# Side B of a decode-attention kernel: tiles of eight heads in 64 KB rows, one transfer a tile

## The chip, the cores and the metric

The kernel runs on one core of a Trainium2 chip. The metric is the device time of one execution, in microseconds. Before the change the median of three runs is 824.88 us (824.64 to 827.48).

## The reference

Two independent attention layers, A and B, each decode one token for 32 heads of 128 values. The two results of 512 values stand side by side in the output. For each side:

```python
q = (x @ wq) split into 32 heads                 # x: 1 x 512, wq: 512 x 4096
scores = einsum("bhqd,bhkd->bhqk", q, k) * 128 ** -0.5
p = softmax(scores)
o = einsum("bhqk,bhkd->bhqd", p, v)
return o reshaped to 1 x 4096 @ wo               # wo: 4096 x 512
```

Everything is bfloat16. Both caches hold 16384 positions a head. A attends to all of them, B to the last W = 4096 only. So A reads 2 x 134 MB of K and V, B 2 x 33.5 MB, and the four weights add 4.2 MB each.

## The kernel before

**Units.** The work is 20 units in the order B0, A0 to A15, B1 to B3; this text numbers them 0 to 19 by place. A unit has an 8.4 MB tile of K and one of V: 128 partitions, each with 256 positions of 128 values, taken as two halves (u = 0, 1) of CH = 128 positions. There are two K buffers (`KS`, alternating) and one V buffer (`VS`).

On side A a unit is two heads; partitions 0 to 63 hold the first, each 256 positions in a row of 64 KB, and one transfer loads the whole tile (`a_pair`, L292). On side B a unit is eight heads, but as two parts of four (`parts` = 2): half u holds heads 4(2g + u) to 4(2g + u) + 3, with partition p = 4i + h holding 128 positions (block i of 32) of head h in a row of 32 KB (`b_window`, L289). Each half is a transfer of its own. Heads lie 4 MiB apart in memory.

**The steps of a unit.** VectorE multiplies each half of K by the head's query (`scores_prod`, L413), adds the 128 values up in a tree of four halvings (`scores_tree`, L425) and a reduction (`scores_sum`, L432), and takes each partition's maximum (`unit_max`, L441). TensorE turns the maxima into a row; VectorE reduces that to one maximum a head (L464) and spreads it again (L465), and TensorE turns it back to a column (`max_all`, L469). ScalarE takes the exponentials (L492) and spreads p over the heads of the tile, one masked copy for each (`spread_p`, L478). TensorE sums the exponentials (`soft_sum`, L520) and multiplies p by V in 64 matmuls (`pv`, L540); ScalarE normalizes them (`evict`, L552); TensorE and ScalarE bring the result into columns (`columns`, L562 and L571). With two parts, side B does the maxima, turns, exponentials and sums for two columns.

**Order.** It is written out by hand in the loop of L687. Unit T's first product stands ahead of the softmax and P·V of unit T - 1, which are put between the steps of unit T. All big loads are issued by SP, in program order: in unit T first V of T - 1 and then K of T + 1, each when its buffer is free. K's buffer is freed by VectorE (`free_k`, L437), V's by ScalarE's copy at L571. Program order and keys decide the semaphores: `_Stream.op` (L71) adds a wait where an operation reads or writes what another wrote or still reads, and the emission is at L120.

**Start.** ScalarE issues six small loads of x (L658). SP loads B's query weights, the first half of unit 0's K, A's query weights and the other half of K (L661 to L664). `spread_x` (L360) copies x, for each of the `nh` heads of a tile, into its share of a zeroed 128-column weight; `project_q` (L386) multiplies with it in groups of 4 x `nh` matmuls and four slots of the query tile, so that each partition gets the query of its own head. B has two such groups, and the copy of each to `q` (L402) has a key of its own, which `scores_prod` names. TensorE takes A's x (`spread_x(A)`) ahead of B's projection.

**End.** The last unit's V is loaded in halves into a free K buffer and into V's (L698, L729), behind A's output weights; B's output weights come last, in five pieces. A's output is projected while VectorE is still at the last unit (L738). The last unit's P·V goes by columns: `pv_columns` (L575) takes V as the weight and 4 columns of p, 128 matmuls for each part, into two PSUM banks, with a normalization after each. The masks for its second half are VectorE's (L483), those for the first ScalarE's. Then `permute_o` (L592) and `project_out_columns` (L624) give B's output.

Of the kernel before, what the change touches and what calls it, by code (L numbers as in the profile page):

```python
# [9 lines left out]
F32 = mybir.dt.float32  # L10
# [193 lines left out]
def kernel(  # L204
# [19 lines left out]
    DN = A_wo.shape[1]  # L224
    KC = D // P
    inv = 1.0 / math.sqrt(DH)
    assert SkA == P // 2 * 2 * CH and WB == P // 4 * CH

    pool = ctx.enter_context(tc.tile_pool(name="pool", bufs=1))
    psum = ctx.enter_context(tc.tile_pool(name="psum", bufs=1, space=bass.MemoryType.PSUM))  # L230
# [1 line left out]
    def sb(name, shape, dtype):  # L232
        return pool.tile(shape, dtype, tag=name, name=name)
# [4 lines left out]
    def flat(t):  # L238
        return t.rearrange("p l d -> p (l d)")
# [2 lines left out]
    VS = sb("v", [P, 2 * CH, DH], BF16)  # L242
    identf = sb("identf", [P, P], F32)
    ident = sb("ident", [P, P], BF16)
    one_f = sb("one_f", [1, 1], F32)
    one_b = sb("one_b", [1, 1], BF16)
    ones_col = sb("ones_col", [P, 1], F32)
    pick = sb("pick", [HQ, P + 4], BF16)
    sc = sb("sc", [P, 2 * CH], F32)
    m_t = sb("m", [P, 2], F32)  # L250
    M_t = sb("M", [1, 8], F32)
    Mr = sb("Mr", [1, 2 * P], F32)
    bias = sb("bias", [P, 2], F32)
    p_t = sb("p", [P, 2 * CH], BF16)
    cs = sb("cs", [P, 2], F32)
    csm = sb("csm", [P, 8], F32)
    pm_t = sb("pm", [P, 2 * CH * 4], BF16)
    r_t = sb("r", [P, 8], F32)
    osb = sb("osb", [P, 512], F32)
    cols = sb("cols", [P, 4], F32)  # L260
# [3 lines left out]
    OC2 = pst("oc2")  # L264

    A, B = _Side(), _Side()
    for s, n, x, wq, wo, nh in ((A, "A", A_x, A_wq, A_wo, 2), (B, "B", B_x, B_wq, B_wo, 4)):
        s.n, s.x, s.wq, s.wo, s.nh, s.parts = n, x, wq, wo, nh, nh // 2
        s.xT = sb(f"xT{n}", [P, KC], BF16)
        s.q = sb(f"q{n}", [P, HQ // nh, DH], BF16)  # L270
        s.O = sb(f"O{n}", [P, HQ], BF16)
        s.Op = sb(f"Op{n}", [P, HQ], BF16)
        s.mask = sb(f"mask{n}", [P, nh], F32)
        s.groups = 4 // s.parts
        s.rows = sb(f"rows{n}", [P, 8 * s.groups // nh, nh, 4], F32)
        s.sel = sb(f"sel{n}", [P, s.parts, nh * 4], F32)
        s.o = pst(f"o{n}")
# [8 lines left out]
            return ap.rearrange("p (h i) -> p h i", h=s.nh)  # L286
        return ap.rearrange("p (i h) -> p h i", h=s.nh)

    def b_window(cache, g):  # L289
        return cache[0, 4 * g : 4 * g + 4, SkB - WB : SkB, :].rearrange("h (i l) d -> i h (l d)", l=CH)  # L290

    def a_pair(cache, g):  # L292
        return cache[0, 2 * g : 2 * g + 2, :, :].rearrange("h (i l) d -> (h i) (l d)", l=2 * CH)
# [16 lines left out]
    def load(dst, src, w, dma, tok=None):  # L310
        st.op("SP", lambda: L.dma_start(out=dst, in_=src), w=w, dma=dma, tok=tok)  # L311

    def load_k_half(un, u):
        load(flat(un.K[:, u * CH : (u + 1) * CH, :]), b_window(B_k_cache, 2 * un.g + u),
             [f"k{un.k}{u}"], f"K{un.k}{u}")

    def load_k(un):
        if un.s is A:
            load(flat(un.K[:, :, :]), a_pair(A_k_cache, un.g), [f"k{un.k}0", f"k{un.k}1"], f"K{un.k}0")
        else:  # L320
            for u in (0, 1):
                load_k_half(un, u)

    def load_v(un):
        if un.s is A:
            load(flat(VS[:, :, :]), a_pair(A_v_cache, un.g), ["v0", "v1"], "V0", "V0")
        else:
            for u in (0, 1):
                load(flat(VS[:, u * CH : (u + 1) * CH, :]), b_window(B_v_cache, 2 * un.g + u),
                     [f"v{u}"], f"V{u}", f"V{u}")  # L330

    def load_wq(s, W, key):
        s.wq_t, s.wq_key = W, key
# [70 lines left out]
    def scores_prod(un, u):  # L404
        s = un.s
        k = un.K[:, u * CH : (u + 1) * CH, :]
        j = un.g if s is A else 2 * un.g + u
        kk = f"k{un.k}{u}"
        ahead = un.g - st.loop["DVE"][1] if st.loop.get("DVE") else None

        def mul(it=None):
            i = j if it is None else it + ahead
            return V.tensor_tensor(  # L413
                out=k, in0=k, in1=s.q[:, bass.ds(i, 1), :].broadcast_to([P, CH, DH]), op=ALU.mult
            )

        st.op("DVE", mul, r=[kk, f"q{s.n}{j // 4}"], w=[kk],
              takes=[f"K{un.k}{u}"] if s is B or u == 0 else [])

    def scores_tree(un, u):  # L420
        k = un.K[:, u * CH : (u + 1) * CH, :]
# [30 lines left out]
    def max_all(un):  # L452
        s, n = un.s, un.s.parts
        w = n * s.nh
        if s is A:
            rows, wide = by_head(s, sm[0:1, 0:P]), by_head(s, Mr[:, 0:P])
            Mv = M_t[:, 0:w]
            spread = Mv.unsqueeze(2).broadcast_to([1, s.nh, P // s.nh])
        else:
            rows = sm[0:1, 0 : n * P].rearrange("p (v i h) -> p v h i", v=n, h=s.nh)  # L460
            wide = Mr[:, 0 : n * P].rearrange("p (v i h) -> p v h i", v=n, h=s.nh)
            Mv = M_t[:, 0:w].rearrange("p (v h) -> p v h", v=n)
            spread = Mv.unsqueeze(3).broadcast_to([1, n, s.nh, P // s.nh])
        st.op("DVE", lambda it=None: V.tensor_reduce(out=Mv, in_=rows, axis=AX.X, op=ALU.max), r=["sm_r"], w=["M"], takes=["smr"])  # L464
        st.op("DVE", lambda it=None: V.tensor_copy(wide, spread), r=["M"], w=["Mr"], tok="Mr")  # L465

        def turn():
            for v in range(n):
                i = T_.matmul(  # L469
                    sm[:, 256 + v : 257 + v], lhsT=Mr[:, v * P : (v + 1) * P], rhs=one_f[:, :],  # L470
                    start=True, stop=True,
                )
            return i

        st.op("PE", turn, r=["Mr", "one_f"], w=["sm_c"], takes=["Mr"], tok="smc")

    def on_scalar(out, in_, mask):
        return S.activation(out=out, in_=in_, func=ACT.Copy, scale=mask)  # L478
# [53 lines left out]
    def pv(un):  # L532
        s, n, g = un.s, un.n // 4, un.s.groups

        def mms():
            for i in range(n):
                for v in range(s.parts):
                    r0 = 32 * (v * g + i % g)
                    l = v * n + i
                    x = T_.matmul(  # L540
                        s.o[r0 : r0 + un.rows, :],
                        lhsT=un.pm[:, l, :, :].rearrange("p a b -> p (a b)"),
                        rhs=VS[:, 4 * l : 4 * l + 4, :],
                        start=(i < g), stop=(i >= n - g),
                    )
            return x

        st.op("PE", mms, r=["v0", "v1"] + [f"pm0.{j}" for j in range(4)], w=["o" + s.n], takes=["V0"] if s is A else ["V0", "V1"], tok="pv")

    def evict(un):  # L550
        s = un.s
# [20 lines left out]

        st.op("ACT", keep, r=["oc", "v0", "v1"], w=[f"O{s.n}.{un.col(0)}"], takes=["oc"], tok="of")

    def pv_columns(un, v, V_t, vk, ps, pk, pmk, takes):  # L575
        s = un.s

        def mms():
            for l in range(un.n):
                x = T_.matmul(  # L580
                    ps[:, 0 : s.nh], lhsT=V_t[:, l, :], rhs=un.pm[:, (v * un.n + l) // 4, :, l % 4],
                    start=(l == 0), stop=(l == un.n - 1),
                )
            return x

        st.op("PE", mms, r=[vk] + [f"{pmk}.{j}" for j in range(4)], w=[pk], takes=takes)
        st.op("DVE", lambda: V.tensor_tensor(  # L587
            out=s.O[:, un.col(v) : un.col(v) + s.nh], in0=ps[:, 0 : s.nh],
            in1=r_t[:, v * s.nh : (v + 1) * s.nh], op=ALU.mult,
        ), r=[pk, "r"], w=[f"O{s.n}.{un.col(v)}"])  # L590

    def permute_o(s):  # L592
        oT = TP[0][0:HQ, 0 : P // 2].bitcast(BF16)
# [57 lines left out]

    wo_pieces = (16, 8, 4, 3, 1)

    x0 = 4 * KC * P
    for s in (B, A):
        s.x_row = flat(KS[1][0:1, :, :])[:, x0 : x0 + D]
        for a, b in ((0, D // 4), (D // 4, D // 2), (D // 2, D)):
# [9 lines left out]
        out=identf[:, :], in_=identf[:, :], compare_op=ALU.not_equal, fill=1.0, base=0,  # L667
        pattern=[[-1, P]], channel_multiplier=1,
    ), r=["identf0"], w=["identf"])
    for t, key, val in ((one_f, "one_f", 1.0), (one_b, "one_b", 1.0), (ones_col, "ones_col", 1.0),  # L670
                        (A.o, "oA", 0.0), (B.o, "oB", 0.0)):
        st.op("DVE", lambda t=t, val=val: V.memset(t[:, :], val), w=[key])
    st.op("DVE", lambda: V.tensor_copy(ident[:, :], identf[:, :]), r=["identf"], w=["ident"])
    spread_x(B, flat(KS[1][:, :, :]), "k10")
    for s in (B, A):
# [6 lines left out]
    project_q(B)  # L682
    project_q(A)
    st.op("SP", lambda: L.dma_start(out=flat(KS[1][:, :, :]), in_=a_pair(A_k_cache, 0)),
          w=["k10", "k11", "xA", "xB"] + [f"k10.{j}" for j in range(4)], dma="K10")

    for T, un in enumerate(units):  # L687
        prev = units[T - 1] if T >= 1 else None
# [4 lines left out]
        if un.last:  # L693
            W, wk = KS[NT % 2], f"k{NT % 2}"
            s = A
            A.wo_t = flat(W[:, 0:CH, :]).rearrange("p (r f) -> p r f", r=HQ)
            load(A.wo_t[:, :, :], A.wo.rearrange("(p r) f -> p r f", r=HQ), [wk + "0"], "woA0")
            load(flat(W[:, CH : 2 * CH, :]), b_window(B_v_cache, 2 * un.g), [wk + "1"], "VL0")  # L698
        both = prev is not None and prev.s is A and un.s is A and prev.g >= 1
        st.loop["DVE"] = ("A", un.g - un.g % 2) if both else None  # L700
        pe = lambda u: {e: ("A", u.g) if u.s is A else None for e in ("PE", "ACT")}
# [24 lines left out]
            st.end_iteration("DVE")  # L726
        st.loop = {}
    un = units[-1]
    load(flat(VS[:, 0:CH, :]), b_window(B_v_cache, 2 * un.g + 1), ["v0"], "VL1")  # L729
    B.wo_t = flat(VS[:, CH : 2 * CH, :]).rearrange("p (r f) -> p r f", r=HQ)  # L730
    src = B.wo.rearrange("(p r) f -> p r f", r=HQ)
    r0 = 0
# [8 lines left out]
    soft(un)  # L741
    soft_sum(un)
    recip(un)
    pv_columns(un, 0, W[:, CH : 2 * CH, :], wk + "1", oc_t, "oc", "pm0", ["pm"])
    pv_columns(un, 1, VS[:, 0:CH, :], "v0", OC2, "oc2", "pm1", ["pm1"])
    parts = [st.ops["PE"][-1]]
    mark = permute_o(B)
    parts += project_out_columns(B, "wo", wo_pieces)
    st.op("SP", lambda: None, r=["outA", "outB"], w=["end"])
# [32 lines left out]
```

## Time and profile before

| | |
|---|---|
| median of 3 runs | 824.88 us |
| the profiled execution | 824.78 us |
| its span | 822.8 us |
| VectorE busy | 762.6 us (93%) |
| TensorE busy, matmuls | 195.1 us (24%) |
| ScalarE busy | 60.0 us (7%) |
| DMA engines busy, main queue | 99.2% of the span |
| read from HBM | 352.32 MB, 428 GB/s over the span |
| mean granted TensorE clock | 0.601 |

The span is the profiled stretch of the core; the time has some 2.0 us around it. A timeline row gives the start in us from the span's start, the time taken, engine, line, operation, what is written from what and the count; in brackets the idle time of the engine ahead of it and what ended that. An engine's name with a q stands for its sequencer; `<-PEq L120` is a wait for a semaphore at L120, where all waits are emitted.

### The profile page before, as it was taken

The page shows a single profiled execution, that of the slowest core. Times are in us where ns is not written, and L with a number is a line of the kernel's source. Part 1 is how long each engine was busy: PE and PEld are TensorE (multiplying, and loading weights), DVE is VectorE, ACT ScalarE, POOL GpSimd, SP SyncE. Part 2 cuts the span into 40 slices and gives each one's busy share as a digit, 9 for nine tenths or more (in the row PEclk, how much of TensorE's full clock was granted, in tenths as well). Part 3 has the DMA queues.
Part 4 walks back from the last instruction along what each step waited for, and adds up shares of the span by engine and source line. Part 5 has one row for each costly group of instructions (what it writes and reads, how often), then busy time and mean ns, then how long its engine had stood idle before and what let it go on. Part 6 is the DMA issues. An engine that isn't in the chain of part 4 may idle for free. (4 is left out here: it accounts for less than half of the span.)

```text
span 822.8 us, 5062 instructions
## 1 busy us (share of the span) xinstructions
PE 195.1 (24%) x1985; PEld 98.4 (12%) x1985; DVE 762.6 (93%) x353; ACT 60.0 (7%) x168; POOL 0.7 (0%) x6
## 2 busy tenths in 40 slices
PE   0700312213030403030312213030303030203175
PEld 0300101101010101010101101010101010101035
DVE  2499999999999999999999999999999999999980
ACT  0101000001010101000000000010100000010110
POOL 0000000000000000000000000000000000000000
PEclk9965656555665556565556565555655565655585
DMA  9999999999999999999999999999999999999997
GB/s 382 433 433 433 452 419 440 427 440 427 440 427 440 427 440 427 440 427 440 427 440 427 440 427 440 427 440 430 436 433 436 430 417 443 424 433 434 434 431 296
DMA packets 8098, 352.50 MB, mean 428 GB/s; under 512 B 915, under 2 KB 1046, under 8 KB 1302
## 3 DMA queue, kind: packets, MB, share of 16 engines
q1 hardware_dynamic: 8072, 352.33, 99.2%
q8 instruction: 9, 0.15, 0.1%
q14 instruction: 3, 0.02, 0.0%
q10 hardware_dynamic: 14, 0.00, 0.0%
HBM read 352.32 MB, written 0.00 MB: 428 GB/s over the span
## 5 line engine op out<-in xcount | busy, mean ns | idle before, releaser
L425 DVE TENSOR_TENSOR k<-k 128x8192 bf16<-128x8192 bf16 (+3 forms) x160 | 344.9, 2156 | 4.8
L413 DVE TENSOR_TENSOR k<-k,qA 128x16384 bf16<-128x16384 bf16 x32 | 277.9, 8684 | 1.7 <-DVEq L120 1.7
L540 PE MATMUL oA<-v,pm 128*8 128x512 bf16 x1024 | 90.5, 531 | 64.4 <-PEq L120 64.4
L447 PE MATMUL sm<-identf,m 128*1 128x128 f32 x24 | 8.1, 370 | 284.4 <-PEq L120 284.4
L413 DVE TENSOR_TENSOR k<-k,qB 128x16384 bf16<-128x16384 bf16 x8 | 69.5, 8685 | 5.6 <-ACT qB L402 5.6
L469 PE MATMUL sm<-one_f,Mr 1*128 1x1 f32 x48 | 12.3, 335 | 168.4 <-PEq L120 168.4
L432 DVE TENSOR_REDUCE sc<-k 128x128 f32<-128x1024 bf16 x40 | 48.8, 1220 | 0.7
L540 PEld LDWEIGHTS oA<-v,pm 128*8 128x8 bf16 x1024 | 30.4, 111 | 117.8 <-issue 110.0
L488 ACT ACTIVATE bias<-sm 128x1 f32<-128x1 f32 (+1 forms) x20 | 3.4, 171 | 468.2 <-ACTq L120 468.2
L447 PEld LDWEIGHTS sm<-identf,m 128*1 128x1 f32 x24 | 1.7, 80 | 286.3 <-issue 286.3
L469 PEld LDWEIGHTS sm<-one_f,Mr 1*128 1x128 f32 x48 | 11.2, 299 | 174.8 <-issue 174.8
L552 ACT ACTIVATE osb<-oA,r 128x512 f32<-128x512 f32 x16 | 11.0, 687 | 168.5 <-ACTq L120 168.5
L562 PE MATMUL oc<-selA,osb 128*128 128x2 f32 x128 | 16.4, 250 | 15.7 <-PEq L120 15.7
L540 PE MATMUL oB<-v,pm 128*16 128x512 bf16 x192 | 16.9, 530 | 13.2 <-PEq L120 13.2
L562 PEld LDWEIGHTS oc<-selA,osb 128*128 128x128 f32 x128 | 15.5, 191 | 23.3 <-issue 23.3
L520 PE MATMUL sm<-cs,rowsA 128*128 128x1 f32 x32 | 8.9, 347 | 32.2 <-PEq L120 32.2
L478 ACT ACTIVATE pm<-p,maskA 128x256 bf16<-128x256 bf16 x32 | 14.5, 500 | 0.5
L520 PEld LDWEIGHTS sm<-cs,rowsA 128*128 128x128 f32 x32 | 8.0, 310 | 33.1 <-issue 33.1
L441 DVE TENSOR_REDUCE m<-sc 128x1 f32<-128x256 f32 (+1 forms) x20 | 8.4, 420 | 3.2 <-DVE sc L432 0.5
L492 ACT ACTIVATE p<-sc,bias 128x256 bf16<-128x256 f32 (+1 forms) x24 | 11.3, 469 | 0.6
L375 DVE CAST xTB<-tp 128x4 bf16<-128x4 f32 x1 | 0.2, 161 | 9.9 <-PE tp L368 9.9
L587 DVE TENSOR_TENSOR OB<-oc,r 128x4 bf16<-128x4 f32 x2 | 0.3, 160 | 9.7 <-PE oc L580 9.7
(73 smaller groups left out, 118.9 us busy)
## 6 DMA issues: line engine op xcount, KB each, us to landing
k<-in_B_k_cache_dram SPq DMA_DIRECT2D x8, 4096.0 KB, 34.3
v<-in_B_v_cache_dram SPq DMA_DIRECT2D x7, 4096.0 KB, 29.7
v<-in_B_wq_dram SPq DMA_DIRECT2D x1, 4096.0 KB, 12.2
v<-in_A_wq_dram SPq DMA_DIRECT2D x1, 4096.0 KB, 30.5
k<-in_A_wo_dram SPq DMA_DIRECT2D x1, 4096.0 KB, 31.1
k<-in_B_v_cache_dram SPq DMA_DIRECT2D x1, 4096.0 KB, 40.4
v<-in_B_wo_dram SPq DMA_DIRECT2D x1, 2048.0 KB, 25.8
v<-in_B_wo_dram SPq DMA_DIRECT2D x1, 1024.0 KB, 27.7
```

The source lines that it names most:

```text
L413: return V.tensor_tensor(out=k, in0=k, in1=s.q[:, bass.ds(i, 1), :].broadcast_to([P, CH, DH]), op=ALU.mult)
L425: st.op("DVE", lambda it=None, w=w: V.tensor_tensor(out=k[:, :, 0:w], in0=k[:, :, 0:w], in1=k[:, :, w : 2 * w], op=ALU.add), r=[kk], w=[kk])
L432: st.op("DVE", lambda it=None: V.tensor_reduce(out=sc[:, u * CH : (u + 1) * CH], in_=k[:, :, 0:8], axis=AX.X, op=ALU.add), r=[f"k{un.k}{u} ...
L441: st.op("DVE", lambda it=None: V.tensor_reduce(out=m_t[:, 0:n], in_=sc[:, :].rearrange("p (v l) -> p v l", v=n), axis=AX.X, op=ALU.max), r ...
L447: i = T_.transpose(sm[0:1, v * P : (v + 1) * P], m_t[:, v : v + 1], identf[:, :])
L469: i = T_.matmul(sm[:, 256 + v : 257 + v], lhsT=Mr[:, v * P : (v + 1) * P], rhs=one_f[:, :], start=True, stop=True,)
L478: return S.activation(out=out, in_=in_, func=ACT.Copy, scale=mask)
L492: st.op("ACT", lambda it=None, v=v: S.activation(out=p_t[:, v * n : (v + 1) * n], in_=sc[:, v * n : (v + 1) * n], func=ACT.Exp, scale=inv, ...
L520: i = T_.matmul(sm[v * w : (v + 1) * w, 264:265], lhsT=s.rows[:, :, :, :].rearrange("p r a b -> p (r a b)"), rhs=cs[:, v : v + 1], start=T ...
L540: x = T_.matmul(s.o[r0 : r0 + un.rows, :], lhsT=un.pm[:, l, :, :].rearrange("p a b -> p (a b)"), rhs=VS[:, 4 * l : 4 * l + 4, :], start=(i ...
L552: st.op("ACT", lambda it=None: S.activation(out=osb[:, :], in_=s.o[:, :], func=ACT.Copy, scale=r_t[:, 0:1]), r=["o" + s.n, "r"], w=["osb"] ...
L562: x = T_.matmul(oc_t[:, 0:w], lhsT=osb[:, j * P : (j + 1) * P], rhs=sel[:, j, :], start=(j == 0), stop=(j == 3),)
```

## The change

Side B's unit becomes one tile of eight heads, laid out like A's rows: partition p = 8i + h holds 256 positions (block i of 16) of head h, 64 KB in a row. The block stays the outermost dimension of the transfer. `parts` is 1 and `nh` 8.

```diff
+    one_f = ones_col[0:1, :]
-    for s, n, x, wq, wo, nh in ((A, "A", A_x, A_wq, A_wo, 2), (B, "B", B_x, B_wq, B_wo, 4)):
-        s.n, s.x, s.wq, s.wo, s.nh, s.parts = n, x, wq, wo, nh, nh // 2
+    for s, n, x, wq, wo, nh in ((A, "A", A_x, A_wq, A_wo, 2), (B, "B", B_x, B_wq, B_wo, 8)):
+        s.n, s.x, s.wq, s.wo, s.nh, s.parts = n, x, wq, wo, nh, 1
...
-    def b_window(cache, g):
-        return cache[0, 4 * g : 4 * g + 4, SkB - WB : SkB, :].rearrange("h (i l) d -> i h (l d)", l=CH)
+    def b_window(cache, g, a=0, b=2 * CH):
+        rows = cache[0, 8 * g : 8 * g + 8, SkB - WB : SkB, :].rearrange("h (i l) d -> i h (l d)", l=2 * CH)
+        return rows[:, :, a * DH : b * DH]
...
     def load_k(un):
-        if un.s is A:
-            load(flat(un.K[:, :, :]), a_pair(A_k_cache, un.g), [f"k{un.k}0", f"k{un.k}1"], f"K{un.k}0")
-        else:
-            for u in (0, 1):
-                load_k_half(un, u)
+        src = a_pair(A_k_cache, un.g) if un.s is A else b_window(B_k_cache, un.g)
+        load(flat(un.K[:, :, :]), src, [f"k{un.k}0", f"k{un.k}1"], f"K{un.k}0")
 
     def load_v(un):
-        if un.s is A:
-            load(flat(VS[:, :, :]), a_pair(A_v_cache, un.g), ["v0", "v1"], "V0", "V0")
-        else:
-            for u in (0, 1):
-                load(flat(VS[:, u * CH : (u + 1) * CH, :]), b_window(B_v_cache, 2 * un.g + u),
-                     [f"v{u}"], f"V{u}", f"V{u}")
+        src = a_pair(A_v_cache, un.g) if un.s is A else b_window(B_v_cache, un.g)
+        load(flat(VS[:, :, :]), src, ["v0", "v1"], "V0", "V0")
...
-        j = un.g if s is A else 2 * un.g + u
+        j = un.g
...
         st.op("DVE", mul, r=[kk, f"q{s.n}{j // 4}"], w=[kk],
-              takes=[f"K{un.k}{u}"] if s is B or u == 0 else [])
+              takes=[f"K{un.k}{u}"] if u == 0 or un is units[0] else [])
...
-    load(flat(VS[:, 0:CH, :]), b_window(B_v_cache, 2 * un.g + 1), ["v0"], "VL1")
+    load(flat(VS[:, 0:CH, :]), b_window(B_v_cache, un.g, CH, 2 * CH), ["v0"], "VL1")
...
-    pv_columns(un, 0, W[:, CH : 2 * CH, :], wk + "1", oc_t, "oc", "pm0", ["pm"])
-    pv_columns(un, 1, VS[:, 0:CH, :], "v0", OC2, "oc2", "pm1", ["pm1"])
+    pv_columns(un, 0, W[:, CH : 2 * CH, :], [(wk + "1", 0, CH)], "pm0", ["pm"])
+    pv_columns(un, CH, VS[:, 0:CH, :], [("v0", 0, CH)], "pm1", ["pm1"])
     parts = [st.ops["PE"][-1]]
+    norm_columns(un)
```

What follows from `parts` = 1 and `nh` = 8 on side B: `m`, `Mr`, `bias` and `cs` have one column; `pm` has room for eight heads; `spread_p` has eight masked copies a unit for four; `spread_x` has eight copies for four into a zeroed area of twice the size, and x's rows lie behind it; `project_q` has one group of 32 matmuls for two of 16, with one copy to `q`. Unit 0's K keeps its two transfers, each with one half of every row, and so does the last unit's V. The last unit's P·V by columns has 8 columns of p in a matmul and runs through all 256 positions into one bank, with one normalization (`norm_columns`) behind both blocks. The order of SP's loads is unchanged but for the merged halves.

More of the change, by code (lines that the diff above doesn't have):

```diff
@@ L226 @@
     inv = 1.0 / math.sqrt(DH)
-    assert SkA == P // 2 * 2 * CH and WB == P // 4 * CH
+    assert SkA == P // 2 * 2 * CH and WB == P // 8 * 2 * CH
     pool = ctx.enter_context(tc.tile_pool(name="pool", bufs=1))
@@ L244 @@
     ident = sb("ident", [P, P], BF16)
-    one_f = sb("one_f", [1, 1], F32)
     one_b = sb("one_b", [1, 1], BF16)
     ones_col = sb("ones_col", [P, 1], F32)
+    one_f = ones_col[0:1, :]
     pick = sb("pick", [HQ, P + 4], BF16)
     sc = sb("sc", [P, 2 * CH], F32)
-    m_t = sb("m", [P, 2], F32)
+    m_t = sb("m", [P, 1], F32)
     M_t = sb("M", [1, 8], F32)
-    Mr = sb("Mr", [1, 2 * P], F32)
-    bias = sb("bias", [P, 2], F32)
+    Mr = sb("Mr", [1, P], F32)
+    bias = sb("bias", [P, 1], F32)
     p_t = sb("p", [P, 2 * CH], BF16)
-    cs = sb("cs", [P, 2], F32)
+    cs = sb("cs", [P, 1], F32)
     csm = sb("csm", [P, 8], F32)
-    pm_t = sb("pm", [P, 2 * CH * 4], BF16)
+    pm_t = sb("pm", [P, 2 * CH * 8], BF16)
     r_t = sb("r", [P, 8], F32)
@@ L313, in load_k_half @@
     def load_k_half(un, u):
-        load(flat(un.K[:, u * CH : (u + 1) * CH, :]), b_window(B_k_cache, 2 * un.g + u),
-             [f"k{un.k}{u}"], f"K{un.k}{u}")
+        a, b = u * CH, (u + 1) * CH
+        load(flat(un.K[:, a:b, :]), b_window(B_k_cache, un.g, a, b), [f"k{un.k}{u}"], f"K{un.k}{u}")
     def load_k(un):
-        if un.s is A:
-            load(flat(un.K[:, :, :]), a_pair(A_k_cache, un.g), [f"k{un.k}0", f"k{un.k}1"], f"K{un.k}0")
-        else:
-            for u in (0, 1):
-                load_k_half(un, u)
-    def load_v(un):
-        if un.s is A:
-            load(flat(VS[:, :, :]), a_pair(A_v_cache, un.g), ["v0", "v1"], "V0", "V0")
-        else:
-            for u in (0, 1):
-                load(flat(VS[:, u * CH : (u + 1) * CH, :]), b_window(B_v_cache, 2 * un.g + u),
-                     [f"v{u}"], f"V{u}", f"V{u}")
+        src = a_pair(A_k_cache, un.g) if un.s is A else b_window(B_k_cache, un.g)
+        load(flat(un.K[:, :, :]), src, [f"k{un.k}0", f"k{un.k}1"], f"K{un.k}0")
+    def load_v(un):
+        src = a_pair(A_v_cache, un.g) if un.s is A else b_window(B_v_cache, un.g)
+        load(flat(VS[:, :, :]), src, ["v0", "v1"], "V0", "V0")
     def load_wq(s, W, key):
@@ L469, in turn @@
                 i = T_.matmul(
-                    sm[:, 256 + v : 257 + v], lhsT=Mr[:, v * P : (v + 1) * P], rhs=one_f[:, :],
+                    sm[:, 256 + v : 257 + v], lhsT=Mr[:, v * P : (v + 1) * P], rhs=one_f,
                     start=True, stop=True,
@@ L473, in turn @@
             return i
-        st.op("PE", turn, r=["Mr", "one_f"], w=["sm_c"], takes=["Mr"], tok="smc")
+        st.op("PE", turn, r=["Mr", "ones_col"], w=["sm_c"], takes=["Mr"], tok="smc")
     def on_scalar(out, in_, mask):
@@ L546, in mms @@
             return x
-        st.op("PE", mms, r=["v0", "v1"] + [f"pm0.{j}" for j in range(4)], w=["o" + s.n], takes=["V0"] if s is A else ["V0", "V1"], tok="pv")
+        st.op("PE", mms, r=["v0", "v1"] + [f"pm0.{j}" for j in range(s.nh)], w=["o" + s.n], takes=["V0"], tok="pv")
     def evict(un):
@@ L573, in columns, with pv_columns, mms, norm_columns @@
         st.op("ACT", keep, r=["oc", "v0", "v1"], w=[f"O{s.n}.{un.col(0)}"], takes=["oc"], tok="of")
-    def pv_columns(un, v, V_t, vk, ps, pk, pmk, takes):
+    def pv_columns(un, l0, V_t, vks, pmk, takes):
         s = un.s
[L578 to L586, printed above, removed]
+        for i, (vk, a, b) in enumerate(vks):
+            def mms(a=a, b=b):
+                for l in range(a, b):
+                    x = T_.matmul(
+                        oc_t[:, 0 : s.nh], lhsT=V_t[:, l, :], rhs=un.pm[:, (l0 + l) // 4, :, l % 4],
+                        start=(l0 + l == 0), stop=(l0 + l == un.n - 1),
+                    )
+                return x
+            st.op("PE", mms, r=[vk] + [f"{pmk}.{j}" for j in range(s.nh)], w=["oc"], takes=takes if i == 0 else ())
+    def norm_columns(un):
+        s = un.s
         st.op("DVE", lambda: V.tensor_tensor(
-            out=s.O[:, un.col(v) : un.col(v) + s.nh], in0=ps[:, 0 : s.nh],
-            in1=r_t[:, v * s.nh : (v + 1) * s.nh], op=ALU.mult,
-        ), r=[pk, "r"], w=[f"O{s.n}.{un.col(v)}"])
+            out=s.O[:, un.col() : un.col() + s.nh], in0=oc_t[:, 0 : s.nh], in1=r_t[:, 0 : s.nh], op=ALU.mult,
+        ), r=["oc", "r"], w=[f"O{s.n}.{un.col()}"])
     def permute_o(s):
@@ L652 @@
     wo_pieces = (16, 8, 4, 3, 1)
-    x0 = 4 * KC * P
+    x0 = B.nh * KC * P
     for s in (B, A):
@@ L669 @@
     ), r=["identf0"], w=["identf"])
-    for t, key, val in ((one_f, "one_f", 1.0), (one_b, "one_b", 1.0), (ones_col, "ones_col", 1.0),
+    for t, key, val in ((one_b, "one_b", 1.0), (ones_col, "ones_col", 1.0),
                         (A.o, "oA", 0.0), (B.o, "oB", 0.0)):
@@ L684 @@
     st.op("SP", lambda: L.dma_start(out=flat(KS[1][:, :, :]), in_=a_pair(A_k_cache, 0)),
-          w=["k10", "k11", "xA", "xB"] + [f"k10.{j}" for j in range(4)], dma="K10")
+          w=["k10", "k11", "xA", "xB"] + [f"k10.{j}" for j in range(B.nh)], dma="K10")
     for T, un in enumerate(units):
@@ L697 @@
             load(A.wo_t[:, :, :], A.wo.rearrange("(p r) f -> p r f", r=HQ), [wk + "0"], "woA0")
-            load(flat(W[:, CH : 2 * CH, :]), b_window(B_v_cache, 2 * un.g), [wk + "1"], "VL0")
+            load(flat(W[:, CH : 2 * CH, :]), b_window(B_v_cache, un.g, 0, CH), [wk + "1"], "VL0")
         both = prev is not None and prev.s is A and un.s is A and prev.g >= 1
```

## The prediction

> **What bounds the kernel now.** I read the page's queue table first, then its chain, then the timeline at both ends.
>
> ```profile
> DVE  2499999999999999999999999999999999999980
> DMA  9999999999999999999999999999999999999997
> q1 hardware_dynamic: 8072, 352.33, 99.2%
> DMA v<-in_B_wo_dram 4%; SPq L734 0%; PE oc L632 0%; SPq L311 0%; PE tp L645 0%; DVE p L647 0%; DVE cols L641 0%; ACT OB L571 0%
> ```
>
> One queue moves 352 MB and keeps the 16 DMA engines busy for 99.2% of the span; the chain that ended last is the landing of B's output weights, the last bytes of that queue. VectorE is nearly as full (762.6 us of 822.8). So a change gains only by making bytes flow faster, by shortening the ends, or it loses by letting the queue run dry.
>
> How fast the bytes flow is read where TensorE waits for a V tile; its P·V then starts at the landing.
>
> ```profile
> 624.53 6.21 PE L540 MATMUL oA<-v,pm 128*8 128x512 bf16 x64 [6.10 <-PEq L120]
> 663.24 4.99 PE L540 MATMUL oA<-v,pm 128*8 128x512 bf16 x52 [6.69 <-PEq L120]
> ...
> 740.87 3.59 PE L540 MATMUL oB<-v,pm 128*16 128x512 bf16 x32 [6.36 <-PEq L120]
> 779.73 5.43 PE L540 MATMUL oB<-v,pm 128*16 128x512 bf16 x64 [6.88 <-PEq L120]
> ```
>
> Between two such starts lie one K tile and one V tile, 16.8 MB. Side A, single transfers of 64 KB rows: 663.24 - 624.53 = 38.71 us (433 GB/s). Side B, four half transfers of 32 KB rows: 38.86 us. So two halves cost about 0.08 us more than one whole tile.
>
> **The transfers.** Six of B's tiles become one transfer each (K of units 17, 18, 19; V of units 0, 17, 18). Unit 0's K and the last unit's V stay in halves. If a B tile then flows as A's does: 6 x 0.08 = 0.5 us less. If the 0.08 came from the number of heads in a tile (two in A, four in B) and not from the halves, eight heads could cost it once more, on all eight of B's tiles: +0.6 us. I take -0.5, since it is row length and number of transfers that become A's.
>
> [...]
>
> **The start: VectorE begins later.**
>
> ```profile
> 25.01 0.29 PE L368 MATMUL tp<-one_b,k 1*128 1x1 bf16 x4 [11.72 <-DMA k<-in_A_x_dram]
> 25.65 8.74 PE L395 MATMUL tp<-v,k 128*128 128x512 bf16 x32 [0.34 <-DVE xTA L375]
> 30.97 0.58 ACT L402 CAST qB<-tp 128x512 bf16<-128x512 f32 x1 [9.35 <-PE tp L395]
> 31.59 8.69 DVE L413 TENSOR_TENSOR k<-k,qB 128x16384 bf16<-128x16384 bf16 x1 [5.56 <-ACT qB L402]
> 34.43 0.58 ACT L402 CAST qB<-tp 128x512 bf16<-128x512 f32 x1 [2.87 <-PE tp L395]
> ```
>
> Before, B's query came in two groups of 16 matmuls; the first product (L413) needs only the first copy, at 30.97. Now all 32 matmuls make one group: the copy that the product needs is the one at 34.43, 3.46 us later. The spreading of x doubles its memset (0.91 us for 1024 words, so about 1.8) and makes eight copies for four (0.73 us together; 0.7 to 1.5). Both lie ahead of 25.01, where TensorE waits for A's x, with VectorE free from 16.4: nothing. If A's x came 8 us earlier, they would be late next.
>
> From then on VectorE never waits: unit starts run 69.41, ..., 720.50, 758.83, 38.3 us apart, against 38.7 to 38.9 for the DMA. So the 3.46 us stay in its stream, less what side B saves: with one maximum a partition and 128 values in place of 256, the reduction at L464 goes as A's (0.27 for 0.41 us) and the spread at L465 too (0.21 for 0.38). That is 0.3 us in each of the three maxima of B (units 0, 17 and 18, each taken inside the unit behind it) that lie ahead of the last unit's scores: 0.9 us. VectorE reaches the last maximum 3.46 - 0.9 = 2.6 us later.
>
> **Does the queue run dry?** A load is issued when VectorE (K) or TensorE and ScalarE (V) free its buffer. K loads land 35.4 us after issue, of which 19.4 are their own transfer: some 16 us of other bytes lie ahead of each, so 3.5 us late is covered. V's closest place is unit 0: its release follows the spreading of p (L478), which now has eight operations for four, of 0.43 us each at the pace there (1.71 for 4): +1.7 us, less 0.5 for one exponential in place of two. With VectorE's delay the next V load goes out near 91.14 + 3.2 + 1.2 = 95.5 us. Ahead of it in the queue are four 4 MB loads and three of 8 MB, at 9.7 and 19.4 us, from about 2 us on: they end near 99. So 3.5 us are left, and the queue doesn't run dry. Late in the run V's release waits for V's own landing (6 to 7 us idle at L540), which hides all of it. B's whole V load behind the queries goes out when both halves are free, 41.4 us, with a K tile still to flow: covered. SP's order of loads is otherwise the same.
>
> **K in one transfer.** The first product now waits for all of K, not half. The last K tile lands one V transfer (19.4 us) ahead of V's 779.73, that is at 760.3; VectorE wanted its first half at 758.83 and now comes 2.9 us later (two of the three savings lie ahead), behind the landing. The delay of the start covers this wait; without it the price would be 1.5 us.
>
> **The end.**
>
> ```profile
> 789.59 8.75 PE L616 MATMUL oc<-k,OpA 128*1 128x512 bf16 x32 [1.66 <-DMA k<-in_A_wo_dram]
> 796.72 0.42 DVE L441 TENSOR_REDUCE m<-sc 128x2 f32<-128x256 f32 x1
> 798.27 0.38 PE L447 MATMUL sm<-identf,m 128*1 128x128 f32 x2
> 801.84 1.26 ACT L478 ACTIVATE pm<-p,maskB 128x128 bf16<-128x128 bf16 x4
> 803.25 3.51 PE L580 MATMUL oc<-pm,k 128*128 128x4 bf16 x128 [0.81 <-PEq L120]
> 809.01 3.58 PE L580 MATMUL oc<-pm,v 128*128 128x4 bf16 x128 [2.26 <-DMA v<-in_B_v_cache_dram]
> 814.19 0.52 PE L632 MATMUL oc<-OpB,v 128*128 128x1 bf16 x14 [0.37 <-ACT OpB L608]
> 818.61 0.58 PE L632 MATMUL oc<-OpB,v 128*128 128x1 bf16 x16 [0.32 <-DMA v<-in_B_wo_dram]
> ```
>
> The maximum comes 2.6 us later, at 799.7. TensorE was busy with A's projection until 798.3, so the transpose moves only 1.5 us, to 799.8. From there to the masks it took 801.84 - 798.27 = 3.6 us. Now there is one transpose, turn, exponential and masked sum in place of two each, and the 0.3 us at L464 and L465 again; I take 2.7, so the masks start near 802.5. Eight spreads of 0.32 (1.26 / 4) to 0.39 us (one alone): 2.5 to 3.1; I take 2.5, their pace in a row. The first block of P·V starts near 805.1 and ends at 808.6. Its matmuls have 8 columns for 4: one column takes 30 ns (98 in 2.98 us), four 27, so nothing; at L616's 0.53 ns a column it would be 0.3 us a block. The second block waits for its data anyway, until 809.0 (0.5 earlier with the queue). So VectorE's lateness ends in this wait of 2.26 us, with 0 to 0.4 us to spare. After it, TensorE has 0.3 us before the last weights land, and the end follows the queue.
>
> **Sum.** Queue -0.5, end +0.1: -0.4 us. The profiled execution took 824.78 us (span 822.8 and 2.0 around), so 824.4; the median of the three runs is 0.1 above it: **824.5 us**.
>
> **The rivals.**
> - *VectorE's lateness surfaces at the end.* Decides once the first P·V block ends after 808.6 to 809.0. If none of the 0.9 us comes back and spreads cost 0.39, the transpose is at 800.7, the masks start at 804.3 (3.6 later, as before) and end at 807.4, the blocks (3.8 each) end at 815.0 instead of 812.6: +2.4, less 0.3 of room: 826.9 us. For it: the room is half a microsecond. Against: the savings are A's own rows. Chance 24%, a sixth of which goes beyond 4 us (A's x landing later).
> - *The eight heads collide in HBM.* Heads lie 4 MiB apart, and eight streams of a block meet at that distance. A halved rate would add 19.4 us to each of eight tiles: +155, 980 us; it decides (0.5%) from 0.5 us, or 2.7%, a tile. Against: A's two and B's four heads, at the same distance, flow within 0.4% of each other. Chance 4%. [...]
> - *Nothing changes in the queue*, since its engines are full either way: 824.9 us. 10%.
> - *Each transfer has a serial cost.* The output's takes 2.6 us from issue (820.18) to the span's end; six of these gone: 809 us. Against: the 0.08 us above. 2%.
> - The forecast: 60%.
>
> Half a percent (4.1 us) is about what a measurement of this kernel can tell from no change. Faster by more: 2%. Slower by more: 4% and 4%. Within: 90%. Range for 8 in 10: from 823.3 (forecast, less 1.2: some half of the 2.6 us by which one of the three runs stands off the median) to 827.5 (the first rival, with +0.6 for the queue).
>
> **What would show it.** K and V of B in one landing, P·V starts 38.7 us apart on B; first product at 35.0 us; VectorE without a wait at L413 in units 17 to 19; the second block of P·V still waiting for V; the DMA row full. A gap in the DMA row, a unit of B longer than 39.5 us, or a second block that waits for the mask or for TensorE instead of the DMA, proves me wrong.

## The result, and the profile after

The changed kernel takes 997.53 us (median of six runs, 996.26 to 999.0) against 825.28 us (six runs, 824.64 to 827.48): ratio 1.2084, 95% interval 1.2071 to 1.2096. The forecast was 824.5 us, so 173 us were missed. The profiled execution took 998.12 us, its span is 996.3.

The page of the changed kernel: DMA's busy share in 40 slices of some 25 us, what it moved in them, the main queue, and the chain that ended last.

```profile
DMA  9999999999999999999999999999999999999997
GB/s 288 283 313 295 211 420 443 432 424 437 445 421 432 447 426 429 442 434 424 432 445 426 432 445 429 424 437 445 258 208 376 210 210 205 206 210 200 268 216 226
q1 hardware_dynamic: 7208, 352.33, 99.4%
DMA v<-in_B_wo_dram 5%; SPq L730 0%; PE oc L628 0%; SPq L312 0%; PE tp L641 0%; DVE p L643 0%; DVE cols L637 0%; ACT OB L565 0%
```

Before the change the flow was, in slices of some 21 us:

```profile
GB/s 382 433 433 433 452 419 440 427 440 427 440 427 440 427 440 427 440 427 440 427 440 427 440 427 440 427 440 430 436 433 436 430 417 443 424 433 434 434 431 296
```

The bound is the same, and so is the busy share: the 16 engines are 99.4% busy with the same 352 MB. But where B's tiles are under way (the first five slices and from the 29th on) the same busy engines move less: 200 to 216 GB/s in nine of these 17 slices, up to 376 in the others, which weights or a tile of A share, instead of some 430. A busy share tells that an engine has a packet, not how fast its bytes flow: in the traces a packet of 64 KB takes 2.42 us before the change (4090 of 4096 under 2.5), and in the changed kernel 742 of them take 4.8 to 5.2 us (B's six whole tiles have 768 packets). The windows view says it for one stretch inside side B (the last three columns: TensorE clock, DMA share, GB/s):

```profile
800.00:860.00 60.00, 7.59 (x77) 4.30 (x77) 37.76 (x16) 4.92 (x13) 0.00 (x0) 0.55 1.00 209
```

TensorE's P·V starts mark the landings as they did before. Here is unit 16's before the change, and then those of units 14 to 18 in the changed kernel:

```profile
702.01 5.04 PE L540 MATMUL oA<-v,pm 128*8 128x512 bf16 x64 [7.24 <-PEq L120]
```

```profile
667.95 6.44 PE L534 MATMUL oA<-v,pm 128*8 128x512 bf16 x64 [6.85 <-PEq L120]
708.82 6.48 PE L534 MATMUL oA<-v,pm 128*8 128x512 bf16 x64 [9.02 <-PEq L120]
770.49 6.37 PE L534 MATMUL oA<-v,pm 128*8 128x512 bf16 x64 [8.99 <-PEq L120]
851.13 5.33 PE L534 MATMUL oB<-v,pm 128*32 128x512 bf16 x64 [25.50 <-PEq L120]
931.68 6.00 PE L534 MATMUL oB<-v,pm 128*32 128x512 bf16 x64 [25.38 <-PEq L120]
```

With one K and one V tile of B between them, 851.13 to 931.68 is 80.55 us, where it was 38.86: one tile costs 40.3 us instead of 19.4. The whole difference can be read off these starts against those of before. At unit 14's V (667.95 for 624.53) it is 43.4 us: unit 0's K and V. At 15 and 16 it has grown by 2.2 and 22.9 (K of unit 17 in between), at 17 and 18 by 41.8 and 41.7 (K and V each), and to the end of the span by 21.5 (the last V): 173.5 us for eight tiles, 21.7 each on average. On side A the pace is unchanged (38.70 us a unit).

VectorE, which waited for K tiles for 1.7 us in all before the change, now stands idle until K lands:

```profile
749.10 8.69 DVE L407 TENSOR_TENSOR k<-k,qB 128x16384 bf16<-128x16384 bf16 x1 [23.48 <-DVEq L120]
810.78 8.69 DVE L407 TENSOR_TENSOR k<-k,qB 128x16384 bf16<-128x16384 bf16 x1 [23.46 <-DVEq L120]
891.44 8.69 DVE L407 TENSOR_TENSOR k<-k,qB 128x16384 bf16<-128x16384 bf16 x1 [42.45 <-DVEq L120]
```

### The profile page after: what moved, and what is told of

Read it like the earlier page. It is cut to its first block, busy times and chain, and to the rows that moved or that the text cites. A ratio compares the mean times of both kernels' runs of the same rounds, so it can differ in the third digit from the quotient of the medians.

```text
span 996.3 us, 5025 instructions
## 1 busy us (share of the span) xinstructions
PE 198.9 (20%) x1967; PEld 99.5 (10%) x1967; DVE 764.6 (77%) x358; ACT 64.2 (6%) x174; POOL 0.7 (0%) x6
## 3 DMA queue, kind: packets, MB, share of 16 engines
q1 hardware_dynamic: 7208, 352.33, 99.4%
## 5 line engine op out<-in xcount | busy, mean ns | idle before, releaser
L407 DVE TENSOR_TENSOR k<-k,qB 128x16384 bf16<-128x16384 bf16 x8 | 69.5, 8688 | 100.5 <-DVEq L120 91.0
L534 PE MATMUL oA<-v,pm 128*8 128x512 bf16 x1024 | 95.9, 556 | 114.2 <-PEq L120 114.2
L463 PE MATMUL sm<-ones_col,Mr 1*128 1x1 f32 x40 | 10.8, 338 | 253.8 <-PEq L120 253.8
L463 PEld LDWEIGHTS sm<-ones_col,Mr 1*128 1x128 f32 x40 | 9.7, 300 | 259.5 <-issue 259.5
L482 ACT ACTIVATE bias<-sm 128x1 f32<-128x1 f32 x20 | 3.4, 171 | 487.3 <-ACTq L120 487.3
L534 PE MATMUL oB<-v,pm 128*32 128x512 bf16 x192 | 16.3, 516 | 76.4 <-PEq L120 76.4
L458 DVE TENSOR_REDUCE M<-sm 1x2 f32<-1x128 f32 (+1 forms) x20 | 5.4, 272 | 22.9 <-DVEq L120 22.9
L534 PEld LDWEIGHTS oB<-v,pm 128*32 128x32 bf16 x192 | 6.9, 125 | 84.6 <-issue 82.9
L472 ACT ACTIVATE pm<-p,maskB 128x256 bf16<-128x256 bf16 (+1 forms) x32 | 12.3, 467 | 0.1
```

Source lines behind the costliest of these rows:

```text
L407: return V.tensor_tensor(out=k, in0=k, in1=s.q[:, bass.ds(i, 1), :].broadcast_to([P, CH, DH]), op=ALU.mult)
L463: i = T_.matmul(sm[:, 256 + v : 257 + v], lhsT=Mr[:, v * P : (v + 1) * P], rhs=one_f, start=True, stop=True,)
L482: st.op("ACT", lambda it=None: S.activation(out=bias[:, 0 : s.parts], in_=sm[:, 256 : 256 + s.parts], func=ACT.Copy, scale=-inv), r=["sm_c ...
L534: x = T_.matmul(s.o[r0 : r0 + un.rows, :], lhsT=un.pm[:, l, :, :].rearrange("p a b -> p (a b)"), rhs=VS[:, 4 * l : 4 * l + 4, :], start=(i ...
```

## Experiments

Two theories could explain a halved flow. **H**: the rows collide where they are read, in HBM, because the heads lie 4 MiB apart (the second rival of the prediction). **S**: the loss comes with the form of the transfer and the partitions it writes, wherever its rows are read. Its outermost dimension was 128 on side A (433 GB/s) and 32 on side B (432 GB/s) before the change, and is 16 now (209 GB/s). Both were the author's guesses at this point. Below, only the sources, the partitions or the number of transfers of a tile are changed. Where no count is given, a time is that of a single run. In the first four, and in the last, only `b_window` differs from the changed kernel; a diff without minus lines replaces the return above it.

### Heads a few KiB nearer

```diff
-        rows = cache[0, 8 * g : 8 * g + 8, SkB - WB : SkB, :].rearrange("h (i l) d -> i h (l d)", l=2 * CH)
-        return rows[:, :, a * DH : b * DH]
+        R = 2 * CH * DH
+        first = cache[0, 0, 0:1, 0:1]
+        return bass.AP(tensor=first.tensor, offset=first.offset + 8 * g * SkB * DH + (SkB - WB) * DH + a * DH,
+                       ap=[[R, 16], [SkB * DH - 2048, 8], [1, (b - a) * DH]])
```

> The changed kernel with the heads of a B tile 4 MiB - 4 KiB apart in its source instead of 4 MiB; sixteen by eight rows of 64 KB into the same partitions as in the changed kernel, so B's data is shifted and its output is not the reference's. Theory H (the rows collide in HBM because heads lie 4 MiB apart, which a few KiB of padding undo): B tiles back at 19.4 us for 8.4 MB, about 825 us in all. [...]

Measured: 997.55 us. Its P·V starts, 80.6 us apart as in the changed kernel:

```profile
850.42 5.40 PE L535 MATMUL oB<-v,pm 128*32 128x512 bf16 x64 [25.55 <-PEq L120]
931.04 6.04 PE L535 MATMUL oB<-v,pm 128*32 128x512 bf16 x64 [25.41 <-PEq L120]
```

### One stretch of memory

```diff
-        return bass.AP(tensor=first.tensor, offset=first.offset + 8 * g * SkB * DH + (SkB - WB) * DH + a * DH,
-                       ap=[[R, 16], [SkB * DH - 2048, 8], [1, (b - a) * DH]])
+        return bass.AP(tensor=first.tensor, offset=first.offset + g * P * R + a * DH,
+                       ap=[[R, 16], [16 * R, 8], [1, (b - a) * DH]])
```

> The changed kernel with each B tile read from one stretch of 8.4 MB: sixteen by eight rows of 64 KB, the eight 1 MiB apart, the sixteen 64 KiB apart; same partitions and same shape of transfer, other data (B's output is not the reference's). Theory H: no two rows 4 MiB apart, so 19.4 us a tile and about 825 us. Theory S: 40 us a tile, about 997 us. If only 4 MiB or only many heads at once matter, it is fast too.

Measured: 997.67 us. Nothing is gained, though all rows lie in one stretch. (Against what the expectation says, rows do lie 4 MiB apart here, the fifth to eighth of a block behind its first to fourth; in the run above the heads do not, and it is as slow.) Theory H has failed in both, and with it any form that needs many heads.

### 128 rows in one dimension, 1 MiB apart

```diff
+        return bass.AP(tensor=first.tensor, offset=first.offset + g * R + a * DH,
+                       ap=[[16 * R, 128], [1, (b - a) * DH]])
```

> The changed kernel with each B tile read as 128 rows of 64 KB in one dimension, 1 MiB apart, so that rows four partitions apart lie 4 MiB apart (other data, B's output is not the reference's). Theory H: at least as slow as the changed kernel, 997 us or more, since now all sixteen engines are 4 MiB apart. Theory S: a transfer with 128 rows outermost is dealt like A's, 19.4 us a tile, about 825 us.

Measured: 831.22 us. The P·V starts of side B are 38.69 us apart, A's pace:

```profile
747.67 5.25 PE L535 MATMUL oB<-v,pm 128*32 128x512 bf16 x64 [4.46 <-PEq L120]
786.36 6.37 PE L535 MATMUL oB<-v,pm 128*32 128x512 bf16 x64 [4.49 <-PEq L120]
```

So rows 1 MiB apart flow at full rate here. The run is some 6 us behind the kernel before by then (747.67 for 740.87, 786.36 for 779.73): 5.0 us stand since unit 1's V (126.39 for 121.43), the rest comes at unit 17's. Their cause is not shown.

### 32 blocks by four heads

```diff
+        return bass.AP(tensor=first.tensor, offset=first.offset + 4 * g * SkB * DH + a * DH,
+                       ap=[[R, 32], [SkB * DH, 4], [1, (b - a) * DH]])
```

> The changed kernel with each B tile read as 32 blocks by four heads, rows of 64 KB, heads 4 MiB apart (the last 8192 positions or others of four heads; B's output is not the reference's). Everything else is the changed kernel. Theory S: with 32 outermost as before the change, 19.4 us a tile; the time then tests the rest of the prediction: 824.5 us, first product near 35.0 us, no waits of VectorE in the last units. Theory H in its form for eight heads: the same; in its form for any heads 4 MiB apart with 64 KB rows: 997 us.

Measured: 826.32 us (ten runs, 824.61 to 827.38) against 825.38 us for the kernel before (thirteen runs): ratio 1.001, interval 1.000 to 1.002. Everything of the change is in it but the 16 outermost and the eight heads in the source (a tile is read from four), and the 173 us are gone. The runs above have already cleared the source. Its two P·V starts on side B:

```profile
740.65 5.48 PE L535 MATMUL oB<-v,pm 128*32 128x512 bf16 x64 [1.33 <-PEq L120]
779.35 4.91 PE L535 MATMUL oB<-v,pm 128*32 128x512 bf16 x64 [1.91 <-PEq L120]
```

### Side A's tiles, named 16 x 8 and 32 x 4 and 64 x 2

These start from the kernel before and touch A's V alone. The three differ in how a tile's 128 rows are named, hardly in where they lie; by the shift of 4 KiB a block the rows no longer lie at one pitch.

```diff
-            load(flat(VS[:, :, :]), a_pair(A_v_cache, un.g), ["v0", "v1"], "V0", "V0")
+            R = 2 * CH * DH
+            first = A_v_cache[0, 2 * un.g, 0:1, 0:1]
+            src = bass.AP(tensor=first.tensor, offset=first.offset, ap=[[8 * R - 2048, 16], [R, 8], [1, R]])
+            load(flat(VS[:, :, :]), src, ["v0", "v1"], "V0", "V0")
```

> The kernel before, with A's sixteen V tiles named as sixteen blocks by eight rows of 64 KB, the blocks 512 KiB - 4 KiB apart so that the two dimensions stay apart (A's V data is shifted by up to 60 KiB, its output is not the reference's). The addresses are A's but for that shift; no heads 4 MiB apart are read otherwise than before. Theory H: 825 us. Theory S: A's V tiles take 40 us instead of 19.4: 16 x 21 = 335 us more, about 1160 us.

> The counterpart: A's sixteen V tiles as 32 blocks by four rows of 64 KB, the blocks 256 KiB - 4 KiB apart (A's V data is shifted by up to 124 KiB, its output is not the reference's). Both theories: 825 us; if it is slow as well, neither the sixteen nor HBM is the cause but that the transfer has two dimensions of rows or that the blocks are unaligned.

> The kernel before with A's V tiles named as 64 blocks by two rows of 64 KB, the blocks 128 KiB - 4 KiB apart (A's V data is shifted by up to 252 KiB, its output is not the reference's). Theory S: an outermost dimension of 64 can be dealt as 32 and 128 are: 825 us. If only 32 and 128 happen to fit, about 1260 us.

Measured: 1257.62, 825.61 and 824.84 us, beside 824.54, 824.54 and 824.68 us for the kernel before. The name alone makes the difference. The size for 16 x 8 was off: 433 us for 16 tiles, 27 each where 21 were expected. The P·V starts are 62.2 us apart in the first units (38.7 before the change) and 67.7 to 69.5 in the last. The timeline of that run shows where the last units lose more:

```profile
656.52 5.15 PE L543 MATMUL oA<-v,pm 128*8 128x512 bf16 x64 [27.69 <-PEq L120]
725.99 4.44 PE L543 MATMUL oA<-v,pm 128*8 128x512 bf16 x40 [28.15 <-PEq L120]
```

```profile
664.05 0.54 SPq L311 DMA_DIRECT2D v<-in_A_v_cache_dram  x1
664.64 0.59 SPq L311 DMA_DIRECT2D k<-in_A_k_cache_dram  x1
```

V lands at 656.5 and its buffer is free for the next at 664.0. Until then SP has issued nothing behind the K tile under way (the next K stands after V in its order), and from 656.5 to 664.0 the DMA's share is 0.12, at 52 GB/s. The queue is not quite dry: two of the 16 engines (0.12 x 16 = 1.9) are still at that K tile, which the others have left by 658.3. The main queue's share of the span is 94.7%.

These two late engines answer a question that the times alone leave open: whether an engine's low rate is its own or comes from the others. The trace does not name engines, but a packet that starts where another ends can be followed. The K tile is named as 128 rows. While the others stand idle, three 64 KB rows of it take 2.42 us on each of the two; from 665.4 us, when the others have begun V's 16 blocks, the last three take 5.1 us each. So here an engine was slowed by what the others did.

### 64 partitions at a time

```diff
-            load(flat(VS[:, :, :]), a_pair(A_v_cache, un.g), ["v0", "v1"], "V0", "V0")
+            src = a_pair(A_v_cache, un.g)
+            load(flat(VS[0:64, :, :]), src[0:64, :], ["v0"], "V0", "V0")
+            load(flat(VS[64:128, :, :]), src[64:128, :], ["v1"], "V1", "V1")
...
```

P·V then waits for both landings.

> The kernel before, with each of A's sixteen V tiles loaded by two transfers of 64 partitions, one head each; same rows, same addresses, all of the computation. [...]

Measured: 1259.77 us, beside 824.54 us for the kernel before. The same rows are read, one head after the other; the lower and the upper half of the partitions are written one after the other, and the flow falls to 181 to 210 GB/s in twelve of the 40 slices (below). A tile costs 27.2 us more (435 us for 16). The next run reads by the same two transfers, but into the even and the odd partitions (`VS[0:128:2]`, `VS[1:128:2]`):

> As the run with A's V in two transfers of 64 partitions, but the first goes to the even and the second to the odd partitions (A's softmax still takes the old places, so its output is not the reference's). Sources, rows and sizes are the same as there, where it took 1260 us. [...] If 64 rows in a transfer are slow by themselves: 1260 us.

Measured: 824.52 us, beside 824.68 us for the kernel before. The flow of the first and the second of these runs, in the same 40 slices:

```profile
GB/s 400 433 434 260 299 235 304 231 329 208 329 221 325 210 329 206 325 204 302 204 319 181 288 210 260 240 202 300 200 296 204 292 204 319 181 263 325 434 431 268
```

```profile
GB/s 382 433 433 433 454 416 441 427 440 427 440 427 440 427 440 427 440 427 440 427 443 424 443 424 443 424 443 424 443 424 443 424 425 441 424 433 434 432 427 302
```

Between these two runs only the partitions differ. So for 64 rows the partitions that are being written decide, and a step of two partitions takes the whole loss away. Why neighbouring partitions lose it, and whether 16 blocks of eight lose theirs in the same way, no run shows.

### Heads outermost

```diff
-        rows = cache[0, 8 * g : 8 * g + 8, SkB - WB : SkB, :].rearrange("h (i l) d -> i h (l d)", l=2 * CH)
+        rows = cache[0, 8 * g : 8 * g + 8, SkB - WB : SkB, :].rearrange("h (i l) d -> h i (l d)", l=2 * CH)
```

> The changed kernel with the eight heads outermost and the sixteen blocks inside, so partition 16 h + i; the steps behind it still take partition 8 i + h, so B's output is not the reference's. If a transfer is dealt over as many engines as its outermost dimension allows, eight engines carry B's tiles: 40 us a tile or more (about 997 us) with the DMA row at half. If all sixteen carry it, theory S has no forecast of its own here.

Measured: 1369.98 us. A stretch inside side B has DMA at a share of 0.51 and 109 GB/s:

```profile
1000.00:1060.00 60.00, 1.11 (x4) 1.00 (x4) 37.76 (x16) 4.08 (x11) 0.00 (x0) 0.50 0.51 109
```

A share of 0.51 is that of eight of the 16 engines at work throughout. Estimated from it, each moves 109 / 8 = 13.6 GB/s, against 433 / 16 = 27.1 at full rate. That is worse than the 997 us that were expected at the least: half of the engines and, on top, each at half its rate.

## Why the prediction was wrong

- **The step that failed is "The transfers".** It had -0.5 us, with bounds of -0.5 and +0.6, and the spans of the profiled executions differ by +173.5. It took row length, number of transfers and number of heads as all that distinguishes B's tile from A's, and left out that the outermost dimension of the transfer went from 32 to 16. The nearest rows, A's 128 and B's 32 by 4, both flow at full rate; an interpolation between them could not bound a third kind. What the runs showed in its place: 16 blocks of eight rows flow at 209 GB/s and cost 40.3 us a tile for 19.4, in each of the three places where B's rows were read (997.53, 997.55 and 997.67 us). The prediction's own sign, a unit of B longer than 39.5 us, came with 80.55. That the queue sets the end was right, so all of it went into the time.
- **The rival "the eight heads collide in HBM"** had nearly the right size (980 us, and 21.7 us a tile for its 19.4) with a chance of 4%, and the wrong mechanism: with the heads moved or the tile in one stretch of memory the time is the same (997.55 and 997.67 us), and with rows 1 MiB apart in one dimension it flows (831.22 us). That the size fits is luck.
- **Row length and merging**: right in the run with 32 x 4. B's pace is 38.70 us a unit for 38.86, the 0.08 us a tile that were counted on. Whether eight heads instead of four cost it once more stays open: no run with eight heads 4 MiB apart flowed at full rate.
- **The start**: right in kind, a little small. In the run with 32 x 4 the first product starts 4.6 us later instead of 3.5:

```profile
35.54 0.58 ACT L397 CAST qB<-tp 128x512 bf16<-128x512 f32 x1 [13.65 <-PE tp L390]
...
36.16 8.69 DVE L408 TENSOR_TENSOR k<-k,qB 128x16384 bf16<-128x16384 bf16 x1 [9.86 <-ACT qB L397]
```

  The 32 matmuls took 9.59 us and began 0.27 us later; the prediction ended them where 32 in two groups had ended (8.74 us). In the changed kernel itself the first product starts at 44.22 us, since A's x lands later there (TensorE waits for it until 33.64 us, 25.01 before); the queue, 173 us longer, hides it.
- **No dry queue, no wait for the whole K tile**: right in the run with 32 x 4. The idle time ahead of the products is 1.7 us on side A as before and none on side B but the 9.9 of the start.
- **The end**: in the run with 32 x 4 the first rival came true in small. The first block of P·V ends at 809.5 (809.0 was the limit), and TensorE's second block has a gap of 1.9 us that no wait in the profile explains:

```profile
806.08 3.56 PE L575 MATMUL oc<-pm,k 128*128 128x8 bf16 x128 [1.77 <-PEq L120]
809.49 1.18 PE L575 MATMUL oc<-pm,v 128*128 128x8 bf16 x39
812.58 2.52 PE L575 MATMUL oc<-pm,v 128*128 128x8 bf16 x89 [1.91 <-issue]
```

  The last reduction follows at 821.15 instead of 819.23. So without the 16 outermost the rest of the change still gives no gain: +0.9 us at the median (the interval of the ratio begins at 1.000), where -0.4 was forecast.

The trigger of the 173 us is shown: 16 blocks outermost, whatever is read. That an engine was slowed by what the others did is shown too (2.42 and 5.1 us a row), and for two transfers of 64 rows that the partitions written decide (1259.77 and 824.52 us). That 16 blocks of eight lose their rate by the partitions as well is the author's inference from these and from the half rate; no run wrote 16 blocks to other partitions. Which rows each engine gets was not seen: the trace does not name the engine of a packet.

None of these versions beats the kernel before. Of the forms tried, those that flow at full rate have 128 rows, or 32 or 64 blocks that fill all partitions, or 64 rows into every other partition; a tile of eight heads with 256 positions a row has only 16 blocks, and four heads to a transfer is the kernel before.

## What to carry to other kernels

In these runs a load's flow followed from its outermost dimension and from the partitions that it wrote, and busy engines were not enough: a DMA share of 1.00 went with 209 GB/s as with 433. For a tile of 128 partitions, name 32 blocks or more outermost (32, 64 and 128 flowed at some 433 GB/s; 16 at 209; eight at 109), do not split it into halves of neighbouring partitions (1259.77 us for 824.54), and measure one transfer of a new shape before a kernel is built on it. When DMA is 99% busy, read GB/s beside the share: the main queue's was 99.2% at 428 GB/s before the change and 99.4% at 354 after it.

## What the runs showed of the hardware

- 8.4 MB into the same 128 partitions took 19.4 or 40.3 us by the way their rows were named.
- A's V tiles in two transfers of 64 partitions: 1259.77 us in all where the 64 are neighbours, 824.52 us where they alternate, beside 824.54 and 824.68 us in one transfer.
- A slow transfer can cost more than its own time: on side A a 16 x 8 tile added 23.5 us to a unit at first, and 29 to 31 later, when for 7.5 us of a unit the DMA's share was 0.12, two engines' worth.
- 64 KB rows of a tile named as 128 rows took 2.42 us while the other engines stood idle and 5.1 us beside 16 blocks of eight.
- 128 rows 1 MiB apart, and four heads 4 MiB apart, were read at full rate (38.69 and 38.70 us a unit).
